# Three tasks moved in a written-out order of a windowed attention with a token-mixing MLP

## The chip, the cores and the metric

The kernel runs on one core of a Trainium2 chip. The time is the device time of one execution in microseconds (us). TensorE (PE), VectorE (DVE), ScalarE (ACT), GpSimd (POOL) and SyncE (SP) each work through a queue of their own in order, and wait for each other by semaphores.

## The reference

Attention with four sink keys and a window of 128 keys, for 4 batches, 8 heads, 768 tokens and 64 columns a head, and behind it a residual MLP that first mixes tokens and then channels:

```python
scores = np.where(is_sink | in_window, q @ k.T / np.sqrt(D), -1e9)
a = softmax(scores)                       # [4, 8, 768, 768]
x = (a @ v) -> [4, 768, 512]
a1 = alpha1 * x + beta1
tok = einsum('ts,bsd->btd', w_tok, a1)    # w_tok [768, 768]
u = x + lam * tok
a2 = alpha2 * u + beta2
ch = maximum(a2 @ w_ch1, 0) @ w_ch2       # [512, 2048], [2048, 512]
out = u + lam * ch
```

## The kernel before

The whole kernel is one program of 1,153 small tasks. A first part of the source describes the tasks (`add(...)`), each with the engines that it may run on, the tasks that it needs and the buffers that it uses. The order in which they are written into the program, the engine of each and the place ("home") of each buffer are fixed lists: `ORDER`, `ENGINES`, `HOMES`. `Plan.emit` walks through `ORDER` and emits task after task, so that the list gives the order on every engine's queue at once. A task's number is its place among the descriptions.

```python
for i in order:
    t = self.tasks[i]
    e = (ACT, DVE, PE, POOL, SP)[int(engines[i])]
```

Batches count from 0 to 3, tokens go in six row tiles of 128 (0 to 5), and the columns are 512. While one batch is in its MLP, the attention of the next one is woven into it, and the loads of the one after that. For a batch the work goes so:

- Attention. q and k are cast, transposed on TensorE and kept as qkT. For each block j of 128 keys, `scores` makes products of 64 rows (S, L608) into one of the two S places for each group of four heads; ScalarE takes their exponential (E, L630); VectorE or GpSimd multiplies or cuts the window's mask (L645, L570); `pv` multiplies with v (L709), and VectorE divides by the sum of the row (L734, L735) into x. x times alpha1 and so on is xh (L753, L756).
- Token mix. `tok` takes, for one row tile, six matmuls of w_tok against the six xh (L840). VectorE adds the result to x (L847), ScalarE or GpSimd casts x to 16 bits (u, L155 or L157). `uTp` transposes u on TensorE, six transposes for a half of the tokens and two of four column blocks (L881), and then alpha2 and beta2 go in on the way to uT, one block on VectorE (L866) and one on ScalarE (L864).
- Channel MLP. `mlp1` makes a block of h with four matmuls (L901), which ScalarE or VectorE evacuates through the maximum (L907, L909) to hT. For batch 0 `mlp2` multiplies hT by w2 in four parts of four matmuls for each row tile (ch, L1086), and VectorE adds the result to x (L1097), which is stored (L1100). For batches 1 to 3 the second product goes in seven partial products of half size (P, L1018), in the manner of Strassen, and is added to x in pieces (L1031, L1049, L1054, L1057); sums of w2 for that are made by L933.

All results of TensorE other than S go into four accumulators of one bank each (kind "d", homes 0 to 3). A task that takes a home waits until the last reader of the buffer that was there is done. In the places of the change the homes are these:

- Batch 0's ch for row tile 4 has home 2, and so has batch 1's tok for row tile 5 after it. Batch 1's transposes uTp for the first half of its tokens have homes 0 and 3; tok for row tiles 3 and 4 come into these after them. For the second half the transposes have homes 1 and 3, into which the h blocks 13 and 14 come.
- Batch 3's tok for row tile 5 has home 2, into which the first half of product P5 for row tile 1 of batch 2 comes. Batch 3's transposes of the second half have homes 0 and 3; home 0 is that of P5 and P3 for row tile 0 of batch 2, which L1031 reads.

The line numbers are those of the profile.

Of the kernel before, what the change touches and what calls it, by code (L numbers as in the profile page):

```python
# [77 lines left out]
def kernel(  # L78
# [119 lines left out]
    for r in range(NR):  # L198
# [43 lines left out]
        451, 440, 452, 639, 453, 417, 319, 640, 309, 648, 446, 649, 320, 447, 418, 323, 321,  # L242
        448, 645, 664, 646, 324, 322, 449, 623, 329, 650, 665, 454, 347, 325, 651, 455, 330,
        652, 348, 326, 462, 456, 463, 464, 459, 656, 457, 327, 458, 659, 627, 460, 657, 662,
        625, 461, 331, 38, 629, 468, 356, 465, 470, 469, 332, 343, 466, 630, 467, 471, 660,
        333, 350, 622, 328, 310, 661, 658, 477, 884, 342, 883, 472, 474, 473, 889, 478, 479,
        671, 486, 475, 490, 476, 487, 344, 666, 491, 663, 483, 480, 484, 485, 488, 482, 481,
        672, 512, 489, 514, 513, 886, 669, 516, 515, 496, 667, 670, 506, 354, 497, 500, 517,
        507, 346, 510, 668, 684, 511, 881, 677, 685, 502, 678, 501, 682, 504, 683, 546, 505,
        686, 524, 503, 547, 334, 680, 520, 916, 525, 526, 687, 521, 628, 910, 544, 527, 631,  # L250
# [20 lines left out]
        807, 814, 990, 808, 841, 991, 987, 988, 839, 989, 842, 992, 845, 840, 843, 846, 822,  # L271
        847, 844, 993, 849, 836, 994, 850, 821, 997, 995, 848, 1000, 835, 998, 855, 1001,
        999, 851, 837, 996, 1002, 859, 838, 1012, 852, 856, 853, 860, 1006, 1013, 1009,
        1007, 1008, 1014, 1003, 863, 1004, 1005, 854, 1015, 1010, 864, 1011, 857, 872, 862,
        869, 1016, 873, 1017, 866, 870, 861, 1021, 1018, 1022, 1023, 878, 858, 1019, 1020,
        1050, 867, 879, 1026, 875, 1027, 1051, 1048, 876, 1030, 1049, 1038, 1031, 1042,
        1039, 1028, 1043, 1034, 1029, 1044, 1052, 1045, 1035, 1046, 1086, 1047, 1053, 1080,
        1087, 1084, 874, 1081, 1064, 1085, 1032, 1065, 1070, 1033, 1068, 1071, 1058, 1024,
# [1017 lines left out]
```

## Time and profile before

| | |
|---|---|
| median of three runs | 268.48 us (267.78 to 268.67) |
| profiled execution | 268.26 us, span 266.3 us |
| TensorE busy (matmul) | 257.6 us, 97% of the span, 2335 matmuls |
| VectorE busy | 196.0 us, 74% |
| ScalarE busy | 140.0 us, 53% |
| GpSimd busy | 113.2 us, 43% |
| DMA | 33.30 MB, mean 125 GB/s |

The span is that of the profiled execution from its first to its last instruction; the execution's own time holds some 2 us more. The lines of the timeline give start and length in us, the engine, the source line, the instruction with the tiles it writes and reads, how many of them were taken together, and in brackets how long the engine had been idle before and what ended that. Matmuls overlap, so that a row of several is shorter than its number times the length of one.

### The profile page before, as it was taken

The page shows a single profiled execution, that of the slowest core. Times are in us where ns is not written, and L with a number is a line of the kernel's source. Part 1 is how long each engine was busy: PE and PEld are TensorE (multiplying, and loading weights), DVE is VectorE, ACT ScalarE, POOL GpSimd, SP SyncE. Part 2 cuts the span into 40 slices and gives each one's busy share as a digit, 9 for nine tenths or more (in the row PEclk, how much of TensorE's full clock was granted, in tenths as well). Part 3 has the DMA queues.
Part 4 walks back from the last instruction along what each step waited for, and adds up shares of the span by engine and source line. Part 5 has one row for each costly group of instructions (what it writes and reads, how often), then busy time and mean ns, then how long its engine had stood idle before and what let it go on. Part 6 is the DMA issues. An engine that isn't in the chain of part 4 may idle for free.

```text
span 266.3 us, 5785 instructions
## 1 busy us (share of the span) xinstructions
PE 257.6 (97%) x2335; PEld 170.8 (64%) x2335; DVE 196.0 (74%) x403; ACT 140.0 (53%) x227; POOL 113.2 (43%) x131
## 2 busy tenths in 40 slices
PE   8999999999999999999999999999999999999993
PEld 8755556675556544565787776667667666667882
DVE  5789898679787748687877976588688974128892
ACT  1389744799967434669773452752760324543000
POOL 7826906979974437134763030064563120000010
PEclk9999999999999999999999999999999999999999
DMA  7999999999186307637430007010000000100217
GB/s 214 212 273 326 231 249 354 369 268 315 44 214 206 79 0 190 186 100 196 86 118 2 0 0 238 2 42 0 2 0 2 0 2 0 39 2 1 98 68 269
DMA packets 43058, 33.30 MB, mean 125 GB/s; under 512 B 26372, under 2 KB 37388, under 8 KB 43032
## 3 DMA queue, kind: packets, MB, share of 16 engines
q1 hardware_dynamic: 31728, 23.34, 29.6%
q10 hardware_dynamic: 7560, 6.32, 7.8%
q0 software_dynamic: 3744, 3.28, 7.7%
q8 instruction: 18, 0.29, 0.5%
q14 instruction: 8, 0.07, 0.1%
HBM read 29.91 MB, written 6.29 MB: 136 GB/s over the span
## 4 chain that ended last, share of the span: by engine, by line
PE 81%; DVE 8%; ACT 5%; DMA 2%; issue 1%; SPq 0%; DVEq 0%; ACTq 0%
PE h L901 29%; PE P L1018 19%; PE tok L840 9%; PE ch L1086 8%; PE pv L709 3%; PE tp L505 3%; PE S L608 3%; PE idle L148 3%; DMA nat<-in_q_dram 2%; ACT uT L864 2%; DVE uT L866 1%; ACT E L630 1%; PE uTp L881 1%; DVE qkT L157 1%; DVE x L735 1%
## 5 line engine op out<-in xcount | busy, mean ns | idle before, releaser
L901 PE MATMUL h<-uT,w1f 128*128 128x384 f16 x512 | 90.4, 326 | 1.1 <-DVE uT L866 0.5
L901 PEld LDWEIGHTS <-w1f 128*128 128x128 f16 x512 | 48.0, 98 | 32.8 <-issue 3.6
L907 ACT ACTIVATE hT<-h 128x384 f16<-128x384 f32 x77 | 36.2, 492 | 35.1 <-PE h L901 29.5
L909 DVE TENSOR_SCALAR hT<-h 128x384 f16<-128x384 f32 x51 | 27.8, 554 | 22.0 <-PE h L901 19.6
L1018 PEld LDWEIGHTS <-hT 128*128 128x128 f16 x408 | 39.3, 98 | 7.3 <-issue 1.0
L630 ACT ACTIVATE E<-S 128x1024 f16<-128x1024 f32 (+1 forms) x39 | 38.2, 1002 | 6.4 <-PE S L608 4.9
L753 POOL TENSOR_TENSOR tm<-x,la_b 128x512 f32<-128x512 f32 x18 | 24.4, 1358 | 28.1 <-DVE x L735 14.7
L840 PE MATMUL tok<-xh,wtokT 128*128 128x512 f16 x144 | 33.3, 379 | 0.3 <-DVE x L1097 0.2
L1018 PE MATMUL P<-w2f,hT 128*128 128x256 f16 x216 | 26.9, 273 | 0.0
L155 ACT COPY qkT<-tp 128x768 f16<-128x768 f16 x24 | 19.0, 800 | 11.8 <-PE tp L505 11.1
L1031 DVE TENSOR_TENSOR x<-x,P 128x256 f32<-128x256 f32 x45 | 18.2, 418 | 9.2 <-PE P L1018 8.8
L1018 PE MATMUL P<-w2s,hT 128*128 128x256 f16 x192 | 23.7, 273 | 0.5 <-DVE x L847 0.4
L155 ACT CAST u<-x 128x512 f16<-128x512 f32 x16 | 9.6, 618 | 27.7 <-DVE x L847 27.3
L840 PEld LDWEIGHTS <-wtokT 128*128 128x128 f16 x144 | 13.8, 97 | 15.5 <-issue 1.1
L1086 PE MATMUL ch<-w2f,hT 128*128 128x512 f16 x96 | 23.4, 380 | 0.0
L1054 POOL TENSOR_TENSOR x<-x,pt 128x256 f32<-128x256 f32 x4 | 3.4, 853 | 46.5 <-DVE pt L1049 46.5
L735 DVE TENSOR_TENSOR x<-pv,rec 128x256 f32<-128x256 f32 x48 | 20.4, 425 | 1.7
L847 DVE TENSOR_TENSOR x<-x,tok 128x512 f32<-128x512 f32 x24 | 16.0, 682 | 4.4 <-PE tok L840 4.1
L709 PEld LDWEIGHTS <-E 128*128 128x128 f16 x328 | 14.9, 97 | 4.9 <-issue 1.1
L709 PE MATMUL pv<-vfs,E 128*128 128x65 f16 x328 | 17.6, 194 | 0.0
L822 POOL TENSOR_TENSOR w2f<-wst_w,lam_b 128x512 f16<-128x512 f32 x12 | 16.9, 1431 | 0.0
L864 ACT ACTIVATE uT<-uTp,ab 128x384 f16<-128x384 f16 x16 | 10.2, 668 | 11.8 <-PE uTp L881 9.7
(131 smaller groups left out, 376.0 us busy)
## 6 DMA issues: line engine op xcount, KB each, us to landing
wst_w<-in_moe_w_ch_dram SPq DMA_DIRECT2D x8, 512.0 KB, 7.1
nat<-in_q_dram SPq DMA_DIRECT2D x10, 384.0 KB, 6.9
nat<-in_k_dram SPq DMA_DIRECT2D x10, 384.0 KB, 5.6
vnat<-in_v_dram SPq DMA_DIRECT2D x14, 256.0 KB, 4.7
out_dram<-x SPq DMA_DIRECT2D x11, 256.0 KB, 2.4
out_dram<-x ACTq DMA_DIRECT2D x10, 256.0 KB, 2.1
wtn<-in_moe_w_tok_dram SPq DMA_DIRECT2D x6, 384.0 KB, 5.9
w1f<-in_moe_w_ch_dram POOLq DMA_DIRECT2D x4, 512.0 KB, 10.5
```

Source lines behind the costliest of these rows:

```text
L155: nc.scalar.copy(o, i)
L630: nc.scalar.activation(eT.t, pS.t[:, :, 0 : n * w].rearrange("p e (i w) -> p e i w", i=n), AF.Exp, scale=scale)
L709: nc.tensor.matmul(po.t[:, hl, :], eT.t[:, e_, off + i, c : c + P], vf[j][:, h, :], start=(r < 2 and n == 0), stop=(n == len(parts) - 1 an ...
L735: nc.vector.tensor_mul(bx.t[:, 4 * G : 4 * G + 4, :], po.t[:, :, 0:D], rec.t.to_broadcast([P, 4, D]))
L753: engine[e].tensor_mul(bt.t, bx.t.rearrange("p h d -> p (h d)"), la1_b)
L840: nc.tensor.matmul(pt.t, wtokT[:, si, ti * P : (ti + 1) * P], hs[si].t, start=(si == 0), stop=(si == NR - 1))
L901: nc.tensor.matmul(ph.t, w1f[:, c, fi * P : (fi + 1) * P], bu.t[:, c, chk * NTOK : (chk + 1) * NTOK], start=(c == 0), stop=(c == NC - 1))
L907: nc.scalar.activation(bh.t[:, fi, :], ph.t, AF.Relu)
L909: nc.vector.tensor_scalar_max(bh.t[:, fi, :], ph.t, 0.0)
L1018: nc.tensor.matmul(pc.t, hh[:, nt * P : (nt + 1) * P], w(fi), start=(first and n_ == 0), stop=(n_ == HF - 1), skip_group_check=True)
L1031: nc.vector.tensor_add(row(bx)[:, cols], row(bx)[:, cols], pc.t)
L1086: nc.tensor.matmul(pc.t, bh.t[:, fi, nt * P : (nt + 1) * P], w2f[:, fi, :], start=(fi == 0), stop=(fi == NF - 1))
```

## The change

Three numbers stand elsewhere in `ORDER`; nothing else differs.

- Task 333 is the last sum of batch 0: x of row tile 4 plus its ch (L1097, VectorE). It stood behind task 467, the L866 of the transposes `uTp1_0_0` of batch 1, and now stands ahead of it. Between the two places in the list lie tasks of other engines too (471: tok of row tile 3; 660: an exp).
- Task 666 is the scores of batch 2 against key block 1, both groups of heads (TensorE, eight weight loads and eight matmuls, L608). It stood ahead of the transposes 483 and 480 of batch 1's second half of tokens, and now stands behind them and behind task 488, the block 1 of h.
- Task 1016 is the token sum of batch 3 for row tile 5 (L847, VectorE). It stood behind task 862, an L1057 of batch 2, and now stands ahead of it.

```diff
@@ -242,9 +242,9 @@
-        625, 461, 331, 38, 629, 468, 356, 465, 470, 469, 332, 343, 466, 630, 467, 471, 660,
-        333, 350, 622, 328, 310, 661, 658, 477, 884, 342, 883, 472, 474, 473, 889, 478, 479,
-        671, 486, 475, 490, 476, 487, 344, 666, 491, 663, 483, 480, 484, 485, 488, 482, 481,
+        625, 461, 331, 38, 629, 468, 356, 465, 470, 469, 332, 343, 466, 630, 333, 467, 471,
+        660, 350, 622, 328, 310, 661, 658, 477, 884, 342, 883, 472, 474, 473, 889, 478, 479,
+        671, 486, 475, 490, 476, 487, 344, 491, 663, 483, 480, 484, 485, 488, 666, 482, 481,
@@ -271,8 +271,8 @@
-        1007, 1008, 1014, 1003, 863, 1004, 1005, 854, 1015, 1010, 864, 1011, 857, 872, 862,
-        869, 1016, 873, 1017, 866, 870, 861, 1021, 1018, 1022, 1023, 878, 858, 1019, 1020,
+        1007, 1008, 1014, 1003, 863, 1004, 1005, 854, 1015, 1010, 864, 1011, 857, 872, 1016,
+        862, 869, 873, 1017, 866, 870, 861, 1021, 1018, 1022, 1023, 878, 858, 1019, 1020,
```

## The prediction

> **What bounds the kernel now.** I read the page first, then the chain of waits, then the timeline of the two stretches that the three moved steps lie in (96 to 113 us and 207 to 224 us), and last each engine's idle time by releaser. The page says that TensorE is the bound over the whole span:
>
> ```profile
> PE 257.6 (97%) x2335; PEld 170.8 (64%) x2335; DVE 196.0 (74%) x403; ACT 140.0 (53%) x227; POOL 113.2 (43%) x131
> ...
> PE 81%; DVE 8%; ACT 5%; DMA 2%; issue 1%; SPq 0%; DVEq 0%; ACTq 0%
> ```
>
> So a change pays by what it does to TensorE's pauses, and nothing else. The granted clock is 9 tenths or more in every slice. A pause shows less in the busy share than it costs, because matmuls overlap: I measure it from start to start. A row of n matmuls that takes T, the last of them m, has the pitch (T - m) / (n - 1): tok (2.75 - 0.379) / 11 = 0.216 us, h (2.44 - 0.326) / 13 = 0.163, P (1.04 - 0.273) / 7 = 0.110, with m from the page's groups. A group of six tok therefore holds TensorE for 1.30 us, four h for 0.65, eight P for 0.87, and twelve transposes for 0.68 (from 107.96 to the h at 108.64).
>
> The first stretch, where batch 0 ends and batch 1's token mix (tok), its transposes (uTp) and its first h lie beside batch 2's attention:
>
> ```profile
> 101.64 1.46 PE L840 MATMUL tok<-xh,wtokT 128*128 128x512 f16 x6
> ...
> 101.98 2.26 POOL L933 TENSOR_TENSOR w2f<-w2f 128x512 f16<-128x512 f16 x2
> ...
> 102.18 0.48 DVE L866 TENSOR_SCALAR uT<-uTp,ab 128x384 f16<-128x384 f16 x1 [0.64 <-ACT uT L864]
> ...
> 102.58 0.68 DVE L1097 TENSOR_TENSOR x<-x,ch 128x512 f32<-128x512 f32 x1
> ...
> 103.17 1.62 DVE L645 TENSOR_TENSOR E<-E,mask 128x1024 f16<-128x1024 f16 x1
> 103.31 2.75 PE L840 MATMUL tok<-xh,wtokT 128*128 128x512 f16 x12 [0.21 <-DVE x L1097]
> ...
> 104.71 2.07 DVE L847 TENSOR_TENSOR x<-x,tok 128x512 f32<-128x512 f32 x3
> ...
> 106.91 0.61 POOL L157 CAST u<-x 128x512 f16<-128x512 f32 x1 [0.19 <-DVE x L847]
> ...
> 107.42 0.61 PE L608 MATMUL S<-qkT 64*128 64x256 f16 x8
> ...
> 107.96 0.84 PE L881 MATMUL uTp<-iden,u 128*128 128x128 f16 x12
> ...
> 109.21 0.86 DVE L866 TENSOR_SCALAR uT<-uTp,ab 128x384 f16<-128x384 f16 x2 [0.81 <-ACT uT L864]
> 109.74 0.81 PE L901 MATMUL h<-uT,w1f 128*128 128x384 f16 x4 [0.29 <-DVE uT L866]
> ...
> 110.11 0.67 ACT L864 ACTIVATE uT<-uTp,ab 128x384 f16<-128x384 f16 x1 [0.94 <-DVE uT L866]
> ...
> 110.83 2.44 PE L901 MATMUL h<-uT,w1f 128*128 128x384 f16 x14 [0.28 <-ACT uT L864]
> ```
>
> Three pauses. Tok from 101.64 is issued by 102.94, the next starts at 103.31, behind L1097: 0.37. H from 108.64 is issued by 109.29, the next starts at 109.74, behind L866: 0.45. That one is issued by 110.39, the next starts at 110.83, behind L864: 0.44. All three are waits for an accumulator to be read: tok of row tile 5 takes the accumulator that L1097 reads, the h at 109.74 and 110.83 take those of the two uTp.
>
> The second stretch, batch 2's last products beside batch 3's token mix:
>
> ```profile
> 217.12 1.04 PE L1018 MATMUL P<-w2f,hT 128*128 128x256 f16 x8
> 217.24 0.69 DVE L1057 TENSOR_TENSOR x<-x,pt 128x512 f32<-128x512 f32 x1
> 217.84 0.68 DVE L847 TENSOR_TENSOR x<-x,tok 128x512 f32<-128x512 f32 x1
> 218.44 0.75 DVE L1031 TENSOR_TENSOR x<-x,P 128x256 f32<-128x256 f32 x2
> 218.57 1.03 PE L1018 MATMUL P<-w2s,hT 128*128 128x256 f16 x8 [0.42 <-DVE x L847]
> ...
> 218.65 0.61 POOL L157 CAST u<-x 128x512 f16<-128x512 f32 x1 [4.98 <-DVE x L847]
> ...
> 219.44 0.83 PE L881 MATMUL uTp<-iden,u 128*128 128x128 f16 x12
> ```
>
> P from 217.12 is issued by 217.99 and the next starts at 218.57, behind L847: 0.58, the largest pause of the second half.
>
> **The change part by part.** No instruction is added or removed, so the sums of busy time stay. The order on ScalarE, GpSimd and SyncE is the same in both kernels; only VectorE's order (two neighbouring pairs swapped) and TensorE's (one block) differ. The moved steps issue no DMA. One wait is new: the next scores of batch 2 wait for TensorE's own earlier scores. They run at 115.07, over 5 us after those, so I cost it at nothing.
>
> *Last sum of batch 0 (L1097, one instruction, 0.68).* It goes ahead of the L866 that starts at 102.18. Its matmuls begin to be issued at 100.54, the last at 101.19; from the last tok of a group to its L847 takes 0.41 us (105.69 to 106.10, the third L847), so the sum can start at 101.59, and VectorE is free from 101.55. It ends at 102.27. The L866 behind it had to wait for ScalarE until 102.15 and is now about 0.04 late; tok of row tile 4, which takes its accumulator, is not issued before 104.2. The tok at 103.31 now follows at 102.94: 0.37 gained on TensorE.
>
> How much of that lasts depends on L645, the mask of E. It alone takes 0.69 (its rows at 112.49 and 113.7); here it took 1.62, beside GpSimd's L933, whose second half runs from 103.09 to 104.24. The Trainium skill, "SBUF — State Buffer", section "Who interferes with whom", says that a VectorE instruction with two SBUF inputs and a GpSimd instruction that reads SBUF exclude each other, and that whichever starts first holds the port for its whole length. The row agrees: 104.24 plus most of 0.69 is the 104.79 at which L645 ended. By the same rule the order of starts decides: L645 would now start at 103.10 (ScalarE's E ends at 103.07) against GpSimd's 103.09. If GpSimd stays first, L645 still ends at 104.79, the three L847 still start at 104.71, 105.31 and, back to back, 105.91 instead of 106.10: 0.19 gained there. If VectorE is first, the third L847 is tied to TensorE alone and starts at 105.73: 0.37. I take GpSimd first, since 103.09 is before 103.10 and its queue is ready; the other end stays in the range.
>
> *Scores of batch 2 (L608, eight weight loads and eight matmuls).* With a drain of 0.096 on either side they hold TensorE from 107.32 to 107.96; they go behind the twelve transposes and the next h. What covered GpSimd's cast of u (106.91 to 107.53) is gone: the transposes now wait for that cast. It ends 0.19 earlier, at 107.34, so the transposes that need it start at 107.39 instead of 107.96, and the h behind them at about 108.00 instead of 108.64. The uT chain follows the transposes, step by step with its old durations and hand-overs: ScalarE L864 at 107.88 (was 108.51), VectorE L866 from 108.59 to 109.06 and 108.98 to 109.45 (were 109.21, 109.61), ScalarE L864 from 109.49 to 110.16 (was 110.11). TensorE: h from 108.00 to 108.65, scores to 109.29, h at 109.30 (its accumulator is free at 109.11, so the scores now fill the pause that stood there), h at 110.20 behind L864, was 110.83. Gain of the two steps together 0.63. Bounds: 0.44, if what counts is only the h at 109.74 (109.30 now), and 0.81 with VectorE first at L645. The scores' own reader, ScalarE's exp, ran at 111.43; the scores are complete by 109.5, so their later place costs nothing; it would from 1.2 us later.
>
> *Token sum of batch 3 (L847, one instruction, 0.68).* It swaps with L1057 (0.69). Tok of row tile 5 was complete at 216.4, so L847 runs from 217.24 to 217.92 and the P held at 218.57 follows its neighbour at 217.99: the pause of 0.58 is gone. But not all of it is gained. The transposes at 219.44 take the accumulator that the second L1031 reads, and VectorE's four instructions from 217.24 to 219.19 are back to back whatever their order. So transposes start at 219.24: 0.20. Everything up to the h at 222.20 hangs on them and moves by 0.20. The rule of the port speaks against this step: L1057 has two SBUF inputs, and GpSimd's cast of u would now fall beside it (218.05) instead of beside L1031. Without the rule the cast lands at 218.66; with it, held to about 218.52, at 219.0 to 219.15. Both are before the 219.24 that L1031 sets, so the sum is 0.20 by either; a cast later than 219.3 would be late one for one.
>
> *Does it last to the end?* After 111 us TensorE's pauses, start to start, come to about 4 us, half of it the drains around scores, and no idle row after 111 us names a DMA as releaser on TensorE, VectorE, ScalarE or GpSimd: their chains start at TensorE, so they move with it. From 223.9 to 261.7 the chain of waits is TensorE alone. I carry all of it.
>
> Sum: 0.63 + 0.20 = 0.83. The profiled execution took 268.26 (span 266.3 and 2.0 around it), so it would take 267.43; it is 0.22 below the median of the three runs, 268.48, and against that median I say 267.65.
>
> **The rivals.**
> - *VectorE gets the port first at L645.* For it: 0.01 us between the two starts, less than I can foresee. Against: GpSimd's instruction is next in its own queue and waits for nobody. It gives 0.81 + 0.20: 267.47.
> - *The DMA that the chain names holds the uT chain.* The chain of waits passes the L866 at 109.61 through a load of q:
>
> ```profile
> 103.57 6.02 DMA nat<-in_q_dram
> ```
>
> If that landing is what released L866, then the second L866, the last L864 and the h at 110.83 stay where they are, the first two steps give nothing, and 0.20 is left: 268.28. Against: that L866 reads transposes and no loaded tile, and it starts 0.08 before the L866 in front of it ends, as back-to-back VectorE instructions do all over the trace.
> - *Slower: the port changes hands in batch 2's attention.* Around 129 us VectorE's mask L645 starts at 129.24 and GpSimd's L753 at 129.48, and L753 took 1.61 where it takes 1.27 alone: VectorE was first by 0.24. If the earlier arrival lets GpSimd in first, that mask takes 1.62 instead of 0.69, and the evacuations queued behind it on VectorE hold back TensorE by up to 0.93. The next mask, at 130.88, is in the same place; both lost cost 1.86, against 0.83 gained: 269.5. It decides from a shift of 0.24 of the one engine against the other. Against: both hang on the same matmuls and move together.
> - *The change does not do what it says*: excluded for the order, which the two programs show; what is left is that the gain is given back, as above.
>
> **How the numbers follow.** A measurement of this kernel can tell about 0.3%, 0.8 us, from no change, and my sum of 0.83 stands on that line. Forecast (0.83 gained): 0.57. VectorE first: 0.17. DMA holds: 0.12. Port changes hands: 0.14. By over 0.3% faster: somewhat over half of the first, nearly all of the second, together 0.54. Slower by over 0.3%: most of the last case, 0.11. The rest is 0.35. The range goes from 267.0 (1.01 gained and the 0.4 by which medians of such runs may differ, from 267.78 to 268.67 in the three shown) to 268.7 (the DMA case with the same 0.4); the likeliest case's own range is 267.2 to 268.1.
>
> **What would show it.** Right: the tok group at 103.31 follows its neighbour without a pause; the h at 109.74 follows the scores; the h at 110.83 comes about 0.6 earlier; the P at 218.57 follows at pitch, and the transposes behind it come a further 0.2 earlier. L645's duration, 1.6 or 0.7, tells the first rival. Wrong: an h at 110.83 that has not moved (DMA case); masks of 1.6 us around 129 us and new pauses there; a GpSimd cast of over 1.2 us at 218; or a gain at 111 us that is smaller at 200 us.

## The result, and the profile after

The changed kernel takes 267.07 us (median of 9 runs, 266.93 to 267.69), the one before 267.80 in the 9 runs beside it (267.65 to 268.67): 0.73 us less, ratio 0.9971 with a 95% interval of 0.9958 to 0.9984. The forecast was 0.83 us less than the median shown to it (267.65 against 268.48). That median was of three runs, which are among the nine here, and two of them are the highest: over all nine it is 0.68 lower. So the gain is what can be compared, not the time.

The profiled executions say more, 268.26 and 266.99. That is not the change's doing alone. Up to the tok of row tile 3 of batch 1, TensorE has the same instructions in the same order in both programs, and yet that tok starts at 101.64 in the profile before and at 101.11 after; over the ten profiles of this study it starts anywhere from 100.82 to 102.16. The shift is there long before the change: the very first tok, of batch 0, starts at 31.12 before and at 30.58 after. So I measure two stretches inside each profile, from start to start, which the beginning of a run cannot enter:

- A, from the tok of row tile 3 of batch 1 to the fifth block of h of batch 1, the one that waited for L864 (101.64 to 110.83 in the profile before);
- B, from the P just ahead of the pause to batch 3's transposes of the second half (217.12 to 219.44).

The differences are taken from the starts in ns, so that they can be 0.01 off those of the printed ones.

| kernel | A | between A and B | B | B to the last matmul |
|---|---|---|---|---|
| before | 9.19 | 106.28 | 2.33 | 42.01 |
| after | 8.56 | 106.28 | 2.31 | 42.01 |

A lost 0.63, B 0.02, and nothing was taken back: 0.65 in all, against 0.73 by the medians and 0.78 by the ratio (0.43 to 1.12 by its interval). TensorE is the bound as before: it is busy for 256.2 us of 265.2, 97% as before, so its share does not show the gain.

The timeline of the changed kernel over stretch A, with start and length in us, engine, line, instruction, count, and the idle time in front:

```profile
101.07 0.69 DVE L1097 TENSOR_TENSOR x<-x,ch 128x512 f32<-128x512 f32 x1
101.11 4.05 PE L840 MATMUL tok<-xh,wtokT 128*128 128x512 f16 x18
...
101.45 2.26 POOL L933 TENSOR_TENSOR w2f<-w2f 128x512 f16<-128x512 f16 x2
...
102.56 1.70 DVE L645 TENSOR_TENSOR E<-E,mask 128x1024 f16<-128x1024 f16 x1 [0.42 <-ACT E L630]
...
104.18 1.87 DVE L847 TENSOR_TENSOR x<-x,tok 128x512 f32<-128x512 f32 x3
...
105.59 1.21 POOL L157 CAST u<-x 128x512 f16<-128x512 f32 x2 [1.88 <-DVE x L847]
...
106.58 1.06 PE L881 MATMUL uTp<-iden,u 128*128 128x128 f16 x12
...
108.22 0.61 PE L608 MATMUL S<-qkT 64*128 64x256 f16 x8
...
108.77 3.99 PE L901 MATMUL h<-uT,w1f 128*128 128x384 f16 x22
...
108.95 0.67 ACT L864 ACTIVATE uT<-uTp,ab 128x384 f16<-128x384 f16 x1 [0.93 <-DVE uT L866]
...
109.67 2.86 PEld L901 LDWEIGHTS <-w1f 128*128 128x128 f16 x18 [0.31 <-issue]
```

All eighteen tok are one row without a pause, since L1097 started with the first of them. The scores stand behind the transposes, and the h follows them. The transposes take 1.06 instead of 0.84: they now wait for the cast of u that ends at 106.80. The row of 22 h holds the last pause, in front of its fifth matmul. There A ends, at 109.67, behind the L864 that ends at 109.62. The row takes 3.99, which is 0.24 more than 21 pitches of 0.163 and one h of 0.33: that is what is left of the pause of 0.44.

Stretch B of the changed kernel:

```profile
215.94 1.04 PE L1018 MATMUL P<-w2f,hT 128*128 128x256 f16 x8
216.07 0.68 DVE L847 TENSOR_TENSOR x<-x,tok 128x512 f32<-128x512 f32 x1
216.67 0.68 DVE L1057 TENSOR_TENSOR x<-x,pt 128x512 f32<-128x512 f32 x1
216.82 1.04 PE L1018 MATMUL P<-w2s,hT 128*128 128x256 f16 x8
216.88 0.94 POOL L157 CAST u<-x 128x512 f16<-128x512 f32 x1 [4.38 <-DVE x L847]
217.45 0.75 DVE L1031 TENSOR_TENSOR x<-x,P 128x256 f32<-128x256 f32 x2
...
218.26 0.83 PE L881 MATMUL uTp<-iden,u 128*128 128x128 f16 x12 [0.40 <-DVE x L1031]
```

The P follows its neighbour at pitch, so the pause of 0.58 is gone. The transposes now have a pause of 0.57 in its place, and its releaser is L1031. That L1031 starts at 217.45, 0.10 behind the end of L1057 (217.35); L1057 itself starts 0.08 before the end of L847, as neighbours on VectorE do that need not wait. What opened a gap of 0.18 on VectorE is what the experiments had to find.

### The profile page after: what moved, and what is told of

The parts are those of the page before. It is cut to its first block, busy times and chain, and to the rows that moved or that the text cites. A ratio compares the mean times of both kernels' runs of the same rounds, so it can differ in the third digit from the quotient of the medians.

```text
span 265.2 us, 5785 instructions
## 1 busy us (share of the span) xinstructions
PE 256.2 (97%) x2335; PEld 169.5 (64%) x2335; DVE 196.6 (74%) x403; ACT 140.0 (53%) x227; POOL 113.5 (43%) x131
## 4 chain that ended last, share of the span: by engine, by line
PE 80%; ACT 7%; DVE 5%; DMA 3%; issue 2%; POOL 1%; POOLq 0%; DVEq 0%; ACTq 0%
PE h L901 29%; PE P L1018 19%; PE tok L840 9%; PE ch L1086 8%; PE pv L709 3%; PE S L608 3%; PE tp L505 3%; DMA n<-in_q_dram 3%; ACT E L630 2%; ACT uT L864 2%; PE uTp L881 2%; ACT wt L805 1%; DVE uT L866 1%; DVE x L847 1%; DVE x L1057 1%
## 5 line engine op out<-in xcount | busy, mean ns | idle before, releaser
L1031 DVE TENSOR_TENSOR x<-x,P 128x256 f32<-128x256 f32 x45 | 18.2, 417 | 9.4 <-PE P L1018 8.8
L1054 POOL TENSOR_TENSOR x<-x,pt 128x256 f32<-128x256 f32 x4 | 3.4, 850 | 46.8 <-DVE pt L1049 46.8
L847 DVE TENSOR_TENSOR x<-x,tok 128x512 f32<-128x512 f32 x24 | 15.9, 680 | 4.3 <-PE tok L840 4.1
L864 ACT ACTIVATE uT<-uTp,ab 128x384 f16<-128x384 f16 x16 | 10.2, 668 | 11.5 <-PE uTp L881 9.4
```

What stands on the lines that cost most here:

```text
L847: nc.vector.tensor_add(xf, xf, pt.t)
```

## The experiments

Eight kernels, each with only the order changed. The diffs show only the numbers around the moved ones, and the ratios are to the kernel before, run beside them.

**First step alone.**

```diff
-        466, 630, 467, 471, 660, 333, 350,
+        466, 630, 333, 467, 471, 660, 350,
```

> Only the first step: the last sum of batch 0 (L1097) ahead of the L866. Two stretches are measured inside the profile, so that the start of a run does not enter: A, from the first tok of row tile 3 of batch 1 (101.64 in the profile before) to the h that waited for L864 (110.83): 9.19 us before, 8.56 after. B, from the P of 217.12 to the transposes of 219.44: 2.32 before, 2.32 after. The prediction's working: the tok behind L1097 starts 0.37 earlier, the scores still cover GpSimd's cast of u, so the 0.37 lasts: A 8.82, B 2.32, 0.37 us less in all (ratio 0.9986). Rival, that a DMA landing releases the last L866 of A: A stays 9.19 and the ratio is 1.000.

Measured: A 8.82, B 2.32, ratio 0.9980 (0.9966 to 0.9993). A and B are to the hundredth what was expected; the DMA does not hold the uT chain.

**Second step alone.**

```diff
-        344, 666, 491, 663, 483, 480, 484, 485, 488, 482,
+        344, 491, 663, 483, 480, 484, 485, 488, 666, 482,
```

> Only the second step: the scores of batch 2 (L608) behind the transposes and the h. Stretch A is 9.19 before and 8.56 after. The prediction's working: the pause in front of the tok stays (0.37), the transposes wait for the cast of u that ends at 107.53 and start 0.4 earlier than behind the scores, and the uT chain with them: A 8.76, 0.43 less (ratio 0.9984). If the cover were worth more than the pause that the scores now fill, A would be 9.19 or longer. B 2.32.

Measured: A 8.77, B 2.33, ratio 0.9980 (0.9953 to 1.0007). The interval takes in no change, so it is A that shows the gain. The scores pay for themselves in the pause in front of the h. 0.37 and 0.43 alone are 0.80, together they give 0.63: with both, the transposes are held by the cast of u, which the first step brings forward by only 0.20 (5.69 instead of 5.89 behind A's start).

**Third step alone.**

```diff
-        857, 872, 862, 869, 1016, 873,
+        857, 872, 1016, 862, 869, 873,
```

> Only the third step: the token sum of batch 3 (L847) ahead of L1057. The prediction's sum was 0.20 less on stretch B (2.12). In the profile after, B did not get shorter: the P follows at pitch, but the first of the two L1031 starts 0.10 behind the end of the L1057 in front of it, where VectorE's instructions otherwise start 0.08 before that end. Theory: that L1031 adds to the x that L1057 has just written, so it waits for the end of L1057, which the L847 between them used to hide: B 2.30 to 2.32, A 9.19, ratio 1.000. Rival, that the prediction's 0.20 is there and the profile after is an exception: B 2.12, ratio 0.9993. Rival, that GpSimd's cast of u, slowed to 0.94 beside L1057, holds the transposes: B as in the theory, but the transposes start right behind the cast.

Measured: A 9.20, B 2.31, ratio 0.9999 (0.9981 to 1.0017). The 0.20 of the prediction is not there. The cast of u ends 1.88 after B's start and the transposes start at 2.31, right behind the second L1031, which ends at 2.26. So the cast does not hold them.

**First two steps without the third.** The two diffs above together.

> The first two steps without the third. Theory: the third step gives 0.02 at most, so this kernel takes what the changed one takes: stretch A 8.56, B 2.32, ratio 0.9971 to 0.9977. Rival (the third step gives its 0.20 in the total): slower than the changed kernel by 0.20, ratio 0.9979 or more.

Measured: A 8.56, B 2.33, 267.46 us, ratio 0.9973 (0.9959 to 0.9986). The changed kernel's gain is that of these two steps; by the ratio alone the rival's 0.9979 would not be excluded, by B it is.

**An instruction between L1057 and the L1031 on the same x.** L1057 (862) adds to x of row tile 5 of batch 2, and so does the first L1031 behind it (873). Edit of the changed kernel; 857 is the L1054.

```diff
-        857, 872, 1016, 862, 869, 873,
+        872, 1016, 862, 857, 869, 873,
```

> The changed kernel with one more step moved on VectorE: the L1054 that stood ahead of the token sum goes between L1057 and the L1031 that adds to the same x. Same instructions, same sum of their times. Theory (wait for the x just written): the wait is hidden behind L1054, the transposes come 0.2 earlier: B 2.12 against 2.32 of the changed kernel, ratio to before 0.9964 where the changed kernel has 0.9971. Rival (the cast of u holds the transposes): the cast now lies beside L1057 and L1054 both and ends no earlier, so B stays 2.32 or grows.

Measured: B 2.53, A 8.56, ratio 0.9979 (0.9967 to 0.9990): 0.22 longer where 0.20 less was expected. The timeline of this kernel says why:

```profile
216.04 0.68 DVE L1057 TENSOR_TENSOR x<-x,pt 128x512 f32<-128x512 f32 x1
216.25 0.94 POOL L157 CAST u<-x 128x512 f16<-128x512 f32 x1 [4.04 <-DVE x L847]
...
216.64 0.83 DVE L1054 TENSOR_TENSOR x<-x,pt 128x256 f32<-128x256 f32 x1
...
217.39 0.74 DVE L1031 TENSOR_TENSOR x<-x,P 128x256 f32<-128x256 f32 x2
...
218.18 0.83 PE L881 MATMUL uTp<-iden,u 128*128 128x128 f16 x12 [0.62 <-DVE x L1031]
```

The gap is gone: L1031 starts 0.08 before the end of L1054 (217.47). But L1054 takes 0.83 where it took 0.42. It has two inputs in SBUF, and the cast of u, held by L1057, had come to its turn; L1054 then stood until the cast was done at 217.19 and ended 0.28 later. 0.18 saved and 0.41 paid are the 0.22 to within rounding. The rival had said that B would stay or grow, and it grew, but not for the rival's reason: the cast was done 0.99 before the transposes started, and they follow the second L1031. The edit was a bad test of the wait, since it put a second instruction of the kind that excludes GpSimd beside the cast.

**The two L1031 in the other order.** Edit of the changed kernel; 870 is the L1031 that frees the transposes' accumulator.

```diff
-        862, 869, 873, 1017, 866, 870, 861,
+        862, 869, 870, 873, 1017, 866, 861,
```

> The changed kernel, with the two L1031 of stretch B in the other order: first the one that frees the transposes' accumulator (its x is another), then the one that adds to the x that L1057 has just written. Theory: the first one needs nothing from L1057 and starts back to back, the second one's wait is hidden behind it; the transposes are then held by the P in front of them and by the cast of u: B 1.80 to 1.85 instead of 2.32, 0.5 less than the changed kernel, ratio to before 0.9953. Rival (the cast of u holds the transposes): B 2.2 or more.

Measured: B 1.79, A 8.56, 267.13 us, ratio 0.9961 (0.9947 to 0.9975).

```profile
217.54 0.68 DVE L1057 TENSOR_TENSOR x<-x,pt 128x512 f32<-128x512 f32 x1
217.69 1.04 PE L1018 MATMUL P<-w2s,hT 128*128 128x256 f16 x8
217.75 0.95 POOL L157 CAST u<-x 128x512 f16<-128x512 f32 x1 [4.38 <-DVE x L847]
218.14 0.74 DVE L1031 TENSOR_TENSOR x<-x,P 128x256 f32<-128x256 f32 x2
...
218.61 0.88 PE L881 MATMUL uTp<-iden,u 128*128 128x128 f16 x12
```

Behind the same L1057, an L1031 on another x starts 0.08 before its end (218.14 against 218.22); in the changed kernel the L1031 on the same x starts 0.10 behind it. The two also read different products, but that of the one that waits was complete by 216.11, over a us before. And behind the other L1031 the same instruction no longer waits: it starts 0.08 before its neighbour's end. So it is the wait for the x just written, 0.18 from case to case. The transposes have a pause of 0.04 left, still behind the L1031 that frees their accumulator (it ends at 218.56). They take 0.88 instead of 0.83, since the cast of u now ends beside them; that gives back 0.05 behind B.

**GpSimd's L933 away from the mask.** Edit of the changed kernel; 342 is the second of the two L933.

```diff
-        884, 342, 883,
+        884, 883,
...
-        628, 910, 544, 527, 631, 532,
+        628, 910, 544, 527, 631, 342, 532,
```

> The changed kernel, with GpSimd's second L933 of stretch A (the one beside the mask L645) moved to an idle place of GpSimd some 18 us later. Theory (the two exclude each other, so that the mask stood still until that L933 ended): the mask takes 0.7 instead of 1.7, the third L847 is tied to TensorE alone and comes 0.18 earlier, and so do the cast of u, the transposes and the uT chain: A 8.38 instead of 8.56. Rival (the mask is slow for another reason, as being the first of its batch): mask 1.6 to 1.7 and A 8.56. GpSimd's later L933 itself hits nobody: the products that need it come over 10 us after.

Measured: A 8.39, B 2.31, ratio 0.9972 (0.9960 to 0.9983).

```profile
102.13 1.15 POOL L933 TENSOR_TENSOR w2f<-w2f 128x512 f16<-128x512 f16 x1
...
103.25 0.69 DVE L645 TENSOR_TENSOR E<-E,mask 128x1024 f16<-128x1024 f16 x1 [0.42 <-ACT E L630]
...
105.87 0.69 DVE L847 TENSOR_TENSOR x<-x,tok 128x512 f32<-128x512 f32 x1 [0.61 <-PE tok L840]
```

The mask takes 0.69, and the third L847 now waits for TensorE instead of for VectorE's own queue. A is 0.17 shorter than in the changed kernel, close to the 0.18 that the prediction set on a mask that does not wait (0.81 instead of 0.63). The ratio is too rough to show it.

**Both edits.**

> The changed kernel with both edits: the two L1031 in the other order, and the second L933 of GpSimd later. Theory: the gains add, as they lie 100 us apart: A 8.38, B 1.80 to 1.85, 0.7 less than the changed kernel and 1.4 less than before, ratio 0.9948. If TensorE's gain is taken back anywhere behind the stretches, the ratio is nearer to 0.9971 while A and B are as said.

Measured: A 8.39, B 1.79, between them 106.28, behind them 42.06, 266.79 us, ratio 0.9952 (0.9934 to 0.9970). By the stretches this is 0.65 less than the changed kernel and 1.29 less than the kernel before, which makes a ratio of 0.9952 as well. The gains add. Expected were 0.7 and 1.4; but the expected A and B come to no more than 1.34, and 0.05 is given back behind B, as with the L1031 alone. It has the lowest ratio of all, though its interval (6 runs) overlaps that of the kernel with the two L1031 alone turned round.

## Why the prediction was right or wrong

- *TensorE's pauses decide, and what is gained lasts to the end*: right. From A to B all ten profiles have 106.27 to 106.29, from B to the last matmul 42.01, and 42.06 with the L1031 turned round.
- *First two steps, 0.63*: right, step by step. The profile after stands 0.53 earlier; with that added back, the third L847 starts at 105.91 (predicted 105.91), the cast of u ends at 107.33 (107.34), the h behind the scores starts at 109.30 (109.30), and the one behind L864 at 110.20 (110.20).
- *GpSimd first at L645*: right. The mask took 1.70 in the changed kernel, with GpSimd's second L933 started 4 ns ahead of it (102.560 and 102.564 in the trace). In the kernels with the first step and that L933 in its place the lead is 1 to 10 ns, less than the working could tell; that it named the right engine was luck. That the two exclude each other, which the Trainium skill states in "SBUF — State Buffer", section "Who interferes with whom", is shown by the kernel with that L933 elsewhere: 0.69.
- *The DMA that the chain of waits names*: wrong as a rival. With the same loads, A became 0.63 shorter, and the chain of waits of the changed kernel passes over this stretch without a DMA: it runs through the mask, two L847, the casts of u, the transposes, L864 and L866.
- *The port changing hands around 129 us*: it did not. The masks there take 0.71 and 0.74 in the profile after.
- *The cast of u beside L1057*: it took 0.94, as the rule has it, and landed 0.44 before the transposes could start; no loss, as predicted.
- *The sum and the time*: with the true 0.02 the sum is 0.65, and 0.18 of the forecast's 0.83 was not there. The measured 0.73 lies between and its interval holds both, so the times alone can't tell the right sum from the wrong one; the stretches can. The time, 267.07, lies 0.07 inside the forecast's range and 0.13 below that of its likeliest case, because the forecast set out from the higher median of three runs. The chances were split at 0.3%; measured are 0.29% (0.16 to 0.42), which leaves that open.
- *Third step, 0.20*: wrong; it gave 0.02. The term that failed is "VectorE's four instructions from 217.24 to 219.19 are back to back whatever their order". They were back to back because L847 stood between L1057 and the L1031 that adds to the x that L1057 writes. That both touch x of row tile 5 of batch 2 could be read from the code; the working took the four for independent.

What this wait costs stood in the profile before, in batch 3:

```profile
257.31 0.69 DVE L1057 TENSOR_TENSOR x<-x,pt 128x512 f32<-128x512 f32 x1
...
257.92 0.77 DVE L1031 TENSOR_TENSOR x<-x,P 128x256 f32<-128x256 f32 x2
...
258.94 0.68 DVE L1057 TENSOR_TENSOR x<-x,pt 128x512 f32<-128x512 f32 x1
259.73 0.42 DVE L1031 TENSOR_TENSOR x<-x,P 128x256 f32<-128x256 f32 x1
```

The first L1057 is on x of row tile 5 and the L1031 behind it on another x, and it starts 0.08 before the end at 258.00. The second L1057 and the L1031 behind it are both on x of row tile 4, and the L1031 starts 0.10 behind the end at 259.63. Its product was complete by 259.10.

## What to carry to other kernels

When an instruction is taken out from between two others of its engine, ask whether the second reads what the first writes: the one in between may have been hiding that wait, and swapping two neighbours then costs on the one side what it gains on the other. When a pause vanishes, look for what holds the next task in line before counting the gain; here the transposes' accumulator took back 0.57 of the 0.58, and serving its reader first gave 0.48, where the moved step had given 0.02. Gains of a few tenths are measured by the distance between two events inside one profile, which repeated here to 0.02 us, while the time of a whole run moved by 0.5 us and more.

## What the runs showed of the hardware

- VectorE mostly starts an instruction 0.08 us before the end of its neighbour when it need not wait for anything, and behind that end when it reads what the neighbour has just written. In the profile before, it is 0.10 behind L1057 and L765, and 0.03 behind L734 (all 48 times), L1031 and L1049. L1057 and L765 read SBUF alone, the other three read an accumulator; whether that makes the difference is not tested.
- VectorE and GpSimd hold each other up in both directions, within a few tenths of a microsecond: beside L1057, GpSimd's cast took 0.94 instead of 0.61, and the L1054 put next to it then took 0.83 instead of 0.42, waiting for that same cast. Moving a two-input instruction of VectorE can so cost as much again as it takes alone.
- With TensorE's instructions up to there in the same order, the start of the tok of row tile 3 of batch 1 moved by 1.33 us between the ten profiles, more than any of the steps was worth. The first tok of batch 0, at 30.31 to 31.65, had moved by as much.
